# Sharing one run of 64x64 matmuls between two batches in linear attention followed by a two-layer MLP

## The chip, the cores and the metric

The kernel runs on one core of one Trainium2 chip. The metric is device time in microseconds (us), of one launch from start to end. A core has five engines that run side by side and wait for one another through semaphores: TensorE (PE in the profile; its weight loads are PEld), VectorE (DVE), ScalarE (ACT), GpSimd (POOL) and SyncE (SP). Here SP issues most of the DMAs, in program order. Matmul results go to PSUM, which the kernel uses as eight banks of 128 partitions by 512 fp32 values. The operands lie in SBUF.

## The reference: what is computed

There are 8 batches and 8 heads, 576 positions, and a head size of 64. First comes linear attention, then a two-layer MLP with a leaky ReLU:

```python
q_s = softmax(q, over d)          # over the 64 values of a position
k_s = softmax(k, over s)          # over the 576 positions of a head
kv  = einsum('bhsd,bhse->bhde', k_s, v)
x   = einsum('bhsd,bhde->bhse', q_s, kv)     # then 4608 tokens x 512
h   = x @ w_in                               # 512 -> 2048
out = maximum(0.01 * h, h) @ w_out           # 2048 -> 512
```

q, k, v, both weights and the result are float32. The kernel multiplies in bf16.

## The kernel before

**MLP.** The 4608 tokens are cut into nine tiles of 512 (t = 0 to 8). In tiles 1 to 8 the first layer has 16 steps j. Each has four matmuls of 512 columns (448 in tile 1) into one bank `ph` (`layer1`, L462), and ACT's Prelu (`leaky`, L471) makes the bf16 tile `gj` of it. The second layer has four sub-tiles of 128 tokens, each of 16 matmuls (`layer2`, L483) into one bank `pout`. DVE copies it to `out_sb` (L477; ACT does so for two sub-tiles of tile 1), and SP stores it with two DMAs (L480). `pout` has two banks (`psO`) and `out_sb` four buffers. All other PSUM tiles, `ph`, `pkv` and `po`, take turns in six banks (`psB`).

**Attention of one batch.** These are the steps:

- `load_all` (L505) issues three DMAs of 1152 KB on SP, for k, q and v. They go to `raw` buffers, of which there are six, enough for two batches. A load has to wait until its buffer was read for the last time.
- `k_tree` (L152) and `k_allmax` (L157 to L177), both on DVE, find the maxima of k over the positions. `k_sub` (L185, POOL) subtracts them and `k_exp` (L193, ACT) writes `ke`.
- `q_max` (L217, DVE), `q_sub` (L248, POOL), `q_exp` (L256, ACT), `q_sum` (L265 and L267, DVE) and `q_norm` (L272, DVE) make the softmax of q. `q_turn` (L430) transposes it by a DMA that SP issues, into `qX`.
- `v_cast` (L205, POOL, twice) writes v as bf16 into `vb`, beside a column of ones that gives the sum for k's softmax.
- `kv` (L286): 72 matmuls in 64x64 pieces of the array, with 65 columns each, into the two banks `pkv`. Row half hh writes bank hh.
- `kd_make` (L304 and L305): DVE takes a reciprocal and multiplies, twice, and leaves `kd` in SBUF.
- `attend_x` (L435): 16 matmuls in 64x64 pieces (`quads`, L411). Part 0 has five of the nine position groups, 320 columns in four banks, and part 1 the other four, 2 x 256 columns in two banks. ACT then casts the six banks into `xT` (`move`, L402), part 0 first. `xT` is the input of the first layer.

**Order of the work.** The order is written out by hand. `at(t, u, ...)` (L494) hangs steps on unit u of tile t, and `run(t, u)` (L499) issues them there. Units 0 to 15 are the steps of the first layer, and units 16 to 31 are groups of four matmuls of the second. A unit of 32 or more goes on into the next tile. So a unit stands for four matmuls of 512 columns. Each engine works through its own list in this order and waits only for its data and buffers. The store of a sub-tile is issued just ahead of the steps on its last unit, 19, 23, 27 or 31.

Batches 0 and 1 have an order of their own, and `plan2` that of batch 2. `plan(b, o)` (L604) serves batches 3 to 7: it starts in tile b - 2 at unit o, which is 27 for batch 3, 22 for batch 4 and 17 for the others. Counted in tiles, `kv(3)` stands at unit 20 of tile 2 and `attend_x(3)` at unit 29 there. For batch 4 these are units 15 and 25 of tile 3, and for batches 5 to 7 units 10 and 20 of tile b - 1. Tile b is the first to read the tokens of batch b, for b from 3 to 7. The loads of batch b stand at unit 2 of tile b - 2.

Of the kernel before, what the change touches and what calls it, by code (L numbers as in the profile page):

```python
# [8 lines left out]
FP32 = mybir.dt.float32  # L9
# [16 lines left out]
def kernel(  # L26
# [9 lines left out]
    nc = tc.nc  # L36
# [3 lines left out]
    B, H, S, D = q.shape  # L40
# [6 lines left out]
    P = 128  # L47
# [19 lines left out]
    psB_pool = ctx.enter_context(tc.tile_pool(name="psB", bufs=6, space=bass.MemoryType.PSUM))  # L67
    psO_pool = ctx.enter_context(tc.tile_pool(name="psO", bufs=2, space=bass.MemoryType.PSUM))
    BANK_TAG = "bank2k"


    def load(src, b, name, cuts):

        t = raw_pool.tile([P, HL, R, D], FP32, name=name, tag="raw")
        flat = src[b].rearrange("h s d -> (h s d)").rearrange(
            "(hl p r d) -> p hl r d", hl=HL, p=P, r=R
        )
        for hs, rs in cuts:
            nc.sync.dma_start(
                out=t[:, hs, rs].rearrange("p h r d -> p h (r d)"),  # L80
                in_=flat[:, hs, rs].rearrange("p h r d -> p h (r d)"),
            )
        return t

    ALLH, ALLR = slice(0, HL), slice(0, R)
# [47 lines left out]
    def k_begin(b):  # L133
        st[b]["ke"] = ke_pool.tile([P, R, HL, D], BF16, name="ke")
        st[b]["kmax"] = mx_pool.tile([P, HL, D], FP32, name="kmax")
        st[b]["kmaxT"] = mx_pool.tile([P, HL * D], FP32, name="kmaxT")
        st[b]["kall"] = mx_pool.tile([P, HL, D], FP32, name="kall")
# [16 lines left out]
    def k_allmax(b):  # L154


        nc.vector.transpose(  # L157
            out=st[b]["kmaxT"], in_=st[b]["kmax"].rearrange("p h d -> p (h d)")
        )
        m2 = small_pool.tile([P, CB, 2], FP32, name="m2")  # L160
        nc.vector.tensor_reduce(
            out=m2[:, :, 0],
            in_=st[b]["kmaxT"].rearrange("p (c j) -> p c j", j=32),
            axis=AX.X,
            op=ALU.max,
        )
        for a in range(4):
            o = a ^ 1
            nc.vector.tensor_reduce(
                out=m2[32 * o : 32 * o + 32, :, 1],  # L170
                in_=m2[32 * a : 32 * a + 32, :, 0:1],
                axis=AX.X,
                op=ALU.max,
            )
        m = small_pool.tile([P, CB], FP32, name="m")
        nc.vector.tensor_reduce(out=m, in_=m2, axis=AX.X, op=ALU.max)
        nc.vector.transpose(  # L177
            out=st[b]["kall"].rearrange("p h d -> p (h d)"),
            in_=m.unsqueeze(2).to_broadcast([P, CB, 32]),
        )  # L180

    def k_sub(eng, b, hs):
        ks = st[b]["k"][:, hs]
        n = hs.stop - hs.start
        eng.tensor_tensor(  # L185
            out=ks,
            in0=ks,
            in1=st[b]["kall"][:, hs].unsqueeze(2).to_broadcast([P, n, R, D]),
            op=ALU.subtract,
        )  # L190
# [17 lines left out]
    def q_begin(b):  # L208
        st[b]["qe"] = qe_pool.tile([P, R, HL, D], BF16, name="qe")
        if b == 0:  # L210
            for gg in range(2):
                st[b]["qT", gg] = qT_pool.tile([P, 2, R, L], BF16, name=f"qT{gg}", tag="qT")

    def q_max(b, rs):
        n = rs.stop - rs.start
        st[b]["qmax", rs.start] = m = small_pool.tile([P, HL, n], FP32, name="qmax")
        nc.vector.tensor_reduce(out=m, in_=st[b]["q"][:, :, rs], axis=AX.X, op=ALU.max)  # L217
# [62 lines left out]
    def kv_half(b, gg, outs):  # L280

        for r in range(R):
            for hh in range(2):
                rows = slice(hh * L, (hh + 1) * L)
                for hp in range(2):
                    nc.tensor.matmul(  # L286
                        outs[hh][hp * D : (hp + 1) * D],
                        lhsT=st[b]["ke"][rows, r, 2 * gg + hp],
                        rhs=vb2[b % 2][rows, r, 2 * gg + hp, 0 : D + 1],
                        start=(r == 0),  # L290
                        stop=(r == R - 1),
                    )

    def kv(b):
        pkv = [psB_pool.tile([P, 2, 66], FP32, name="pkv", tag=BANK_TAG) for _ in range(2)]
        for gg in range(2):
            kv_half(b, gg, [p[:, gg, 0 : D + 1] for p in pkv])
        st[b]["pkv"] = pkv

    def kd_make(b):  # L300
        for hh in range(2):
            pkv = st[b]["pkv"][hh]
            krec = small_pool.tile([P, 2, 1], FP32, name="krec")
            nc.vector.reciprocal(out=krec, in_=pkv[:, :, D : D + 1])  # L304
            nc.vector.tensor_tensor(  # L305
                out=kd2[b % 2][:, 2 * hh : 2 * hh + 2],
                in0=pkv[:, :, 0:D],
                in1=krec.to_broadcast([P, 2, D]),
                op=ALU.mult,
            )  # L310
# [89 lines left out]
    def move(eng, o, i):  # L400
        if eng is nc.scalar:
            eng.copy(out=o, in_=i)  # L402
        else:
            eng.tensor_copy(out=o, in_=i)

    def quads(b, gg, ps, src, shape=None):

        for hp in range(2):
            for hh in range(2):
                o = ps[hp][hh * D : (hh + 1) * D]  # L410
                nc.tensor.matmul(  # L411
                    o if shape is None else shape(o),
                    lhsT=kd2[b % 2][hp * D : (hp + 1) * D, 2 * hh + gg],
                    rhs=src(hh)[hp * D : (hp + 1) * D],
                    start=True,
                    stop=True,
                )
# [14 lines left out]
            in_=st[b]["qe"][:, rs].rearrange("p r h d -> p (r h d)"),  # L432
        )

    def attend_x(b, parts, engs):  # L435

        qX = st[b]["qX"].rearrange("c (r g) (h l) -> c g h r l", g=2, h=2)
        made = []
        for i in parts:
            rs = XR[i]  # L440
            n = (rs.stop - rs.start) * L
            cols = slice(b * S + rs.start * L, b * S + rs.stop * L)
            per = 512 // n
            for g0 in range(0, 2, per):
                ps = [psB_pool.tile([P, per, n], FP32, name="po", tag=BANK_TAG) for _ in range(2)]
                for gg in range(g0, g0 + per):
                    quads(
                        b,
                        gg,
                        [p[:, gg - g0] for p in ps],  # L450
                        lambda hh: qX[:, gg, hh, rs],
                        lambda o: o.rearrange("p (r l) -> p r l", l=L),
                    )
                for hp in range(2):
                    c = 2 * g0 + hp
                    made.append((xT[:, c : c + 2 * per - 1 : 2, cols], ps[hp]))
        for i, (o, p) in enumerate(made):
            move(engs[i % len(engs)], o, p)
# [35 lines left out]
    def at(t, u, *fns):  # L494
        while t > 0 and u >= 32:
            t, u = t + 1, u - 32
        hooks.setdefault((t, u), []).extend(fns)
# [7 lines left out]
    def load_all(b):  # L505
        whole = [(ALLH, ALLR)]
        st[b]["k"] = load(k, b, "k_raw", whole)
        st[b]["q"] = load(q, b, "q_raw", whole)
        st[b]["v"] = load(v, b, "v_raw", whole)
# [87 lines left out]
    for i in range(2):  # L597
        at(0, (45, 46)[i], lambda i=i: attend_x(1, (i,), (nc.scalar, nc.vector)))


    for b in range(3, B):
        at(b - 2, 2, lambda b=b: load_all(b))

    def plan(b, o):  # L604
        t = b - 2
        at(t, o, lambda: k_begin(b), lambda: q_begin(b), lambda: k_tree(b, ALLH))
        at(t, o + 3, lambda: k_allmax(b), lambda: k_sub(nc.gpsimd, b, ALLH))
        at(t, o + 7, lambda: q_max(b, ALLR), lambda: q_sub(nc.gpsimd, b, ALLR))
        at(t, o + 11, lambda: k_exp(b, ALLH))
        at(t, o + 12, lambda: v_cast(nc.gpsimd, b, 0), lambda: v_cast(nc.gpsimd, b, 1))  # L610
        at(t, o + 16, lambda: q_exp(b, ALLR))
        at(t, o + 18, lambda: q_sum(b, ALLR))
        at(t, o + 21, lambda: q_norm(b, ALLR))
        kvu, pu = o + 25, o + (33 if b == 3 else 34)
        at(t, kvu, lambda: kv(b))
        at(t, kvu + 1, lambda: kd_make(b))
        at(t, o + 22, lambda: q_turn(b))
        at(t, pu + 1, lambda: attend_x(b, (0, 1), (nc.scalar,)))


    def plan2():
# [15 lines left out]

    plan2()
    for b in range(3, B):
        plan(b, {3: 27, 4: 22}.get(b, 17))  # L640


    def g_tile():
# [57 lines left out]
    for t in range(1, NT):  # L701
# [9 lines left out]
        for tsub in range(NTS):  # L711
            row0 = t * TT + tsub * P
            if row0 == T - P:
                for os, copy in ((slice(0, 384), nc.scalar.copy), (slice(384, O), nc.vector.tensor_copy)):
                    po = psB_pool.tile([P, os.stop - os.start], FP32, name="pout2", tag=BANK_TAG)
# [4 lines left out]
            po = psO_pool.tile([P, O], FP32, name="pout")  # L720
# [37 lines left out]
```

## Time and profile before

| what | value |
|---|---|
| time, median of 3 runs | 285.16 us (284.78 to 285.27) |
| the profiled execution's own time | 284.93 us |
| its span, first to last instruction | 283.1 us |
| TensorE clock granted | 1.00 over the span |
| DMA | 46.38 MB, 164 GB/s on average |
| matmuls of layer 1 (L462) | 628 in the trace, 126.8 us busy |
| matmuls of layer 2 (L483) | 579 in the trace, 126.0 us busy |
| kv (L286) | 576 matmuls, 6.5 us busy |
| attend by qX (L411) | 112 matmuls, 269 to 320 ns each by the model |

The span is what the instructions take; the rest of the profiled execution's time lies around it. In the first tile of the profile TensorE also computes matmuls on zeros (L316), 26 of them. The layers have 640 and 592 weight loads (PEld) in the trace, so a few matmul records are missing there; a hole of about 0.216 us between two matmuls with no releaser is such a record. Where a view lists a group, the columns are busy time, the mean of one in ns, and the idle time of the engine just before, with what ended it. In a timeline the first column is the start within the span, and the second the length of a merged group.

The tiles begin, by the first L462 of each, at 50.49 (tile 1), 78.21, 107.53, 136.72, 165.90, 195.06, 224.23 and 251.85 us (tile 8).

### The profile page before, as it was taken

To read this page: it belongs to the slowest core of one execution; us is meant where nothing else is said; L and a number is where in the kernel's file an instruction comes from. 1 tells how busy PE (TensorE), PEld (TensorE's weight loads), DVE (VectorE), ACT (ScalarE), POOL (GpSimd) and SP (SyncE) were. 2 spreads that over 40 slices of the span, in tenths; PEclk is the share of its full clock that TensorE was granted. 3 is DMA by queue.
4 is the path that set the end of the run, shared out by engine and by line. 5 is a ranking of instruction groups with operands and counts; after the bars stand their busy time and mean duration, and the time that the engine had idled before them with its cause. 6 is when DMAs were issued, how large, how long until landed. Compare 5 with 4: busy or idle time off the path is not lost.

```text
span 283.1 us, 4910 instructions
## 1 busy us (share of the span) xinstructions
PE 272.0 (96%) x1967; PEld 131.4 (46%) x1994; DVE 143.6 (51%) x232; ACT 146.0 (52%) x262; POOL 82.7 (29%) x61
## 2 busy tenths in 40 slices
PE   7699899999999999999999999999999999999995
PEld 2277644554444444444444444444444444444443
DVE  3996794987860992597193718472711100110011
ACT  4977881685269208914773367435843165016400
POOL 2523651026078029307800690059000000000000
PEclk9999999999999999999999999999999999999999
DMA  7998999999959166953597349923061310230033
GB/s 251 331 211 313 296 194 165 400 311 355 175 130 411 45 147 157 407 93 74 116 397 150 74 81 380 200 65 80 5 86 39 80 32 0 59 80 13 0 74 74
DMA packets 38870, 46.38 MB, mean 164 GB/s; under 512 B 18240, under 2 KB 21568, under 8 KB 38848
## 3 DMA queue, kind: packets, MB, share of 16 engines
q1 hardware_dynamic: 35456, 41.75, 52.1%
q0 software_dynamic: 3232, 4.19, 8.4%
q8 instruction: 15, 0.25, 0.4%
q10 hardware_dynamic: 160, 0.13, 0.1%
q14 instruction: 7, 0.06, 0.1%
HBM read 36.70 MB, written 9.44 MB: 163 GB/s over the span
## 4 chain that ended last, share of the span: by engine, by line
PE 86%; DMA 7%; issue 1%; DVE 1%; POOL 0%; SPq 0%; POOLq 0%
PE pout L483 44%; PE ph L462 38%; DMA w_out_sb<-in_moe_w_out_dram 3%; DMA w_in_sb<-in_moe_w_in_dram 2%; PE pkv L286 2%; DMA k_raw<-in_k_dram 2%; PE po L411 2%; DVE k_raw L353 1%; SPq L515 0%; POOL gate L580 0%; DVE out_sb L477 0%; POOL gate L547 0%; POOLq L580 0%; POOLq L547 0%
## 5 line engine op out<-in xcount | busy, mean ns | idle before, releaser
L483 PE MATMUL pout<-w_out_sb,gj 128*128 128x512 bf16 (+2 forms) x579 | 126.0, 373 | 2.0 <-issue 1.0
L462 PE MATMUL ph<-xT,w_in_sb 128*128 128x512 bf16 (+3 forms) x628 | 126.8, 357 | 0.9 <-DMA w_in_sb<-in_moe_w_in_dram 0.2
L471 ACT ACTIVATE gj<-ph 128x512 bf16<-128x512 f32 (+2 forms) x152 | 83.5, 581 | 55.5 <-PE ph L462 52.6
L462 PEld LDWEIGHTS <-w_in_sb 128*128 128x128 bf16 x640 | 62.1, 98 | 62.5 <-issue 0.9
L483 PEld LDWEIGHTS <-gj 128*128 128x128 bf16 x592 | 56.2, 98 | 67.0 <-issue 2.8
L477 DVE COPY out_sb<-pout 128x512 f32<-128x512 f32 (+1 forms) x34 | 22.7, 676 | 88.1 <-PE pout L483 66.0
L185 POOL TENSOR_TENSOR k_raw<-k_raw,kall 128x2304 f32<-128x2304 f32 x5 | 25.4, 5070 | 73.8 <-DVE kall L177 44.4
L402 ACT CAST xT<-po 128x320 bf16<-128x320 f32 (+2 forms) x45 | 17.8, 487 | 47.1 <-PE po L411 47.1
L248 POOL TENSOR_TENSOR q_raw<-q_raw,qmax 128x2304 f32<-128x2304 f32 (+3 forms) x10 | 29.7, 2978 | 21.5 <-DMA out_dram<-out_sb 15.4
L265 DVE TENSOR_REDUCE qsum<-qe 128x36 f32<-128x2304 bf16 (+4 forms) x11 | 19.8, 1797 | 30.7 <-ACT qe L256 30.7
L193 ACT ACTIVATE ke<-k_raw 128x2304 bf16<-128x2304 f32 (+2 forms) x11 | 17.5, 1595 | 9.6 <-POOL k_raw L185 9.6
L272 DVE TENSOR_TENSOR qe<-qe,qrec 128x2304 bf16<-128x2304 bf16 (+4 forms) x12 | 21.9, 1826 | 0.4
L217 DVE TENSOR_REDUCE qmax<-q_raw 128x36 f32<-128x2304 f32 (+4 forms) x11 | 19.6, 1791 | 1.4 <-DMA q_raw<-in_q_dram 1.4
L256 ACT ACTIVATE qe<-q_raw 128x2304 bf16<-128x2304 f32 (+4 forms) x11 | 16.8, 1527 | 0.9 <-POOL q_raw L248 0.8
L205 POOL CAST vb<-v_raw 128x1152 bf16<-128x1152 f32 x13 | 14.6, 1153 | 0.0
L152 DVE TENSOR_TENSOR t<-k_raw 128x1024 f32<-128x1024 f32 (+1 forms) x10 | 10.1, 1006 | 0.9 <-DMA k_raw<-in_k_dram 0.7
L152 DVE TENSOR_TENSOR t<-t 128x256 f32<-128x256 f32 (+2 forms) x20 | 9.6, 478 | 0.6
L316 PE MATMUL pout<-zero 128*128 128x512 bf16 x26 | 8.4, 453 | 1.3 <-POOL zero L101 1.3
L477 ACT COPY out_sb<-pout 128x512 f32<-128x512 f32 (+1 forms) x3 | 1.6, 543 | 14.2 <-PE pout L483 14.2
L286 PEld LDWEIGHTS <-ke 64*64 64x64 bf16 x576 | 5.5, 106 | 4.4 <-ACT gj L471 1.7
L286 PE MATMUL pkv<-vb,ke 64*64 64x65 bf16 x576 | 6.5, 194 | 0.8 <-ACT vb L203 0.8
L230 ACT ACTIVATE qe<-q_raw,nmax 128x64 bf16<-128x64 f32 x16 | 5.3, 333 | 3.3 <-DVE nmax L225 3.3
(53 smaller groups left out, 85.8 us busy)
## 6 DMA issues: line engine op xcount, KB each, us to landing
out_dram<-out_sb SPq DMA_DIRECT2D x70, 128.0 KB, 2.4
q_raw<-in_q_dram SPq DMA_DIRECT2D x7, 1152.0 KB, 8.6
v_raw<-in_v_dram SPq DMA_DIRECT2D x7, 1152.0 KB, 11.5
k_raw<-in_k_dram SPq DMA_DIRECT2D x6, 1152.0 KB, 6.1
k_raw<-in_k_dram SPq DMA_DIRECT2D x4, 576.0 KB, 5.2
w_in_sb<-in_moe_w_in_dram POOLq DMA_DIRECT2D x4, 512.0 KB, 7.7
v_raw<-in_v_dram SPq DMA_DIRECT2D x2, 576.0 KB, 7.2
w_out_sb<-in_moe_w_out_dram POOLq DMA_DIRECT2D x4, 256.0 KB, 9.4
```

What stands on the lines that cost most here:

```text
L152: nc.vector.tensor_tensor(out=o, in0=i0, in1=i1, op=ALU.max)
L185: eng.tensor_tensor(out=ks, in0=ks, in1=st[b]["kall"][:, hs].unsqueeze(2).to_broadcast([P, n, R, D]), op=ALU.subtract,)
L217: nc.vector.tensor_reduce(out=m, in_=st[b]["q"][:, :, rs], axis=AX.X, op=ALU.max)
L248: eng.tensor_tensor(out=qs, in0=qs, in1=st[b]["qmax", rs.start].unsqueeze(3).to_broadcast([P, HL, n, D]), op=ALU.subtract,)
L265: nc.vector.reduce_sum(out=qsum, in_=st[b]["qe"][:, rs], axis=AX.X)
L272: nc.vector.tensor_tensor(out=qes, in0=qes, in1=st[b]["qrec", rs.start].unsqueeze(3).to_broadcast([P, n, HL, D]), op=ALU.mult,)
L286: nc.tensor.matmul(outs[hh][hp * D : (hp + 1) * D], lhsT=st[b]["ke"][rows, r, 2 * gg + hp], rhs=vb2[b % 2][rows, r, 2 * gg + hp, 0 : D + 1 ...
L402: eng.copy(out=o, in_=i)
L462: nc.tensor.matmul(ph, lhsT=w_in_sb[:, i, j * P : (j + 1) * P], rhs=xT[:, i, c0 : c0 + n], start=(i == 0 and first), stop=(i == NB - 1 and ...
L471: nc.scalar.activation(out=o, in_=ph, func=AF.Prelu, alpha=LEAKY_SLOPE)
L477: copy(out=out_sb, in_=pout)
L483: nc.tensor.matmul(pout, lhsT=g_sb[j // 2][:, j % 2, tsub * P : (tsub + 1) * P], rhs=w_out_sb[:, j, os], start=(j == 0), stop=(j == NF - 1),)
```

## The change

The products of keys and values of batch b + 1 are issued within `attend_x` of batch b, ahead of its quads, for b = 3 to 6. They lie in the same two banks as the first pair of `po`: columns 0 to 319 hold the query products and columns 320 to 451 hold `pkv`. `attend_x` of batches 3 to 7 stands at unit 29 of tile b - 1, and `kd_make` of the next batch one unit later. `kv(3)` keeps its own place. The preparation of batches 4 to 7 begins at unit 4 of tile b - 2; batch 3 keeps unit 27 of tile 1. The k_sub of batch 4 is on DVE, all four heads in one instruction, and no longer on POOL. The loads of batches 4 to 7 stand at unit 18 of tile 1, unit 12 of tile 2, unit 24 of tile 3 and unit 24 of tile 4.

```diff
-    def kv(b):
-        pkv = [psB_pool.tile([P, 2, 66], FP32, name="pkv", tag=BANK_TAG) for _ in range(2)]
+    def kv(b, pkv=None):
+        if pkv is None:
+            pkv = [psB_pool.tile([P, 2, 66], FP32, name="pkv", tag=BANK_TAG) for _ in range(2)]
...
-    def attend_x(b, parts, engs):
+    def attend_x(b, parts, engs, kv_next=None):
...
-                ps = [psB_pool.tile([P, per, n], FP32, name="po", tag=BANK_TAG) for _ in range(2)]
+                banks = [psB_pool.tile([P, 512], FP32, name="po", tag=BANK_TAG) for _ in range(2)]
+                ps = [p[:, 0 : per * n].rearrange("p (g n) -> p g n", g=per) for p in banks]
+                if kv_next is not None and not pkv:
+                    pkv = [p[:, n : n + 132].rearrange("p (g e) -> p g e", g=2) for p in banks]
+                    kv(kv_next, pkv)
...
     for b in range(3, B):
-        at(b - 2, 2, lambda b=b: load_all(b))
+        at(*{3: (1, 2), 4: (1, 18), 5: (2, 12)}.get(b, (b - 3, 24)), lambda b=b: load_all(b))
...
-        at(t, o + 3, lambda: k_allmax(b), lambda: k_sub(nc.gpsimd, b, ALLH))
+        at(t, o + 3, lambda: k_allmax(b), lambda: k_sub(nc.vector if b == 4 else nc.gpsimd, b, ALLH))
...
-        kvu, pu = o + 25, o + (33 if b == 3 else 34)
-        at(t, kvu, lambda: kv(b))
-        at(t, kvu + 1, lambda: kd_make(b))
+        if b == 3:
+            at(t, o + 25, lambda: kv(b))
+            at(t, o + 26, lambda: kd_make(b))
         at(t, o + 22, lambda: q_turn(b))
-        at(t, pu + 1, lambda: attend_x(b, (0, 1), (nc.scalar,)))
+        after = None if b == B - 1 else b + 1
+        at(b - 1, 29, lambda: attend_x(b, (0, 1), (nc.scalar,), after))
+        if after:
+            at(b - 1, 30, lambda: kd_make(after))
...
-        plan(b, {3: 27, 4: 22}.get(b, 17))
+        plan(b, 27 if b == 3 else 4)
```

More of the change, by code (lines that the diff above doesn't have):

```diff
@@ L433, in q_turn @@
         )
-    def attend_x(b, parts, engs):
+    def attend_x(b, parts, engs, kv_next=None):
         qX = st[b]["qX"].rearrange("c (r g) (h l) -> c g h r l", g=2, h=2)
-        made = []
+        made, pkv = [], []
         for i in parts:
```

## The prediction

> **What bounds the kernel now.** First the page's busy row, then the table of TensorE's waits (total us, times, longest):
>
> ```profile
> PE 272.0 (96%) x1967; PEld 131.4 (46%) x1994; DVE 143.6 (51%) x232; ACT 146.0 (52%) x262; POOL 82.7 (29%) x61
> ```
>
> ```profile
> PE pout L483 <- issue: 1.0, 6, 0.2
> PE kT L327 <- DVE kmax L152: 0.8, 1, 0.8
> PE pkv L286 <- ACT vb L203: 0.8, 1, 0.8
> ```
>
> TensorE is busy 96% of the span. Its waits are short: "issue" is no wait for another engine, and the others, on lines of batch 0's own attention, belong to the start-up. So after the first tile only TensorE's own stream can be shortened. Next the windows, one per token tile (tiles 2 to 5, and tile 7, which carries no attention):
>
> ```profile
> 78.20:107.50 29.30, 28.88 (x213) 13.43 (x216) 19.59 (x32) 14.86 (x25) 14.30 (x5) 1.00 0.61 182
> 107.50:136.70 29.20, 28.94 (x214) 13.43 (x216) 16.13 (x24) 17.43 (x26) 16.00 (x6) 1.00 0.63 179
> ...
> 224.20:251.90 27.70, 27.54 (x127) 12.55 (x129) 2.77 (x4) 9.55 (x16) 0.00 (x0) 1.00 0.17 38
> ```
>
> The first number behind the stretch is its length, then busy time of PE, PEld, DVE, ACT, POOL, and the clock, 1.00 everywhere. A tile with one kv and one attend takes 1.5 us longer (29.2 against 27.7), and that is all that attention costs after the start. The timeline splits it:
>
> ```profile
> 95.61 1.03 PE L483 MATMUL pout<-w_out_sb,gj 128*128 128x512 bf16 x4
> ...
> 96.56 0.69 PEld L286 LDWEIGHTS <-ke 64*64 64x64 bf16 x72 [0.42 <-issue]
> 96.56 0.81 PE L286 MATMUL pkv<-vb,ke 64*64 64x65 bf16 x72
> ...
> 97.30 0.76 PEld L483 LDWEIGHTS <-gj 128*128 128x128 bf16 x5
> ```
>
> ```profile
> 105.17 0.68 PE L411 MATMUL po<-qX,kd 64*64 64x320 bf16 x16
> 105.54 2.39 ACT L402 CAST xT<-po 128x320 bf16<-128x320 f32 x6 [11.89 <-PE po L411]
> ...
> 107.53 1.24 PE L462 MATMUL ph<-xT,w_in_sb 128*128 128x512 bf16 x5
> ```
>
> Matmul starts are measured and ends modelled, so I work with starts. The four L483 ahead of kv(3) start 0.216 us apart, the last at 96.26; the first kv matmul follows it by 0.309. **Entering** a run of 64x64 matmuls thus costs 0.309 - 0.216 = 0.093 us; the other kv and attend runs of tiles 1 to 6 give 0.093 or 0.094. The last kv matmul starts at 97.16 and the next 128x128 weight load at 97.30, 0.14 us later; in the runs of batches 5 to 7 the next matmul comes 0.126 to 0.144 after the last one. Less 0.027 for its own 65 columns (0.216 x 65/512), **leaving** costs 0.10 to 0.12. Leaving an attend costs 0.09 (0.20 us from the last 256-column matmul of batch 2, less 0.108). No engine appears as a releaser in these places: what is lost is the change of shape itself.
>
> **Part 1: kv of the next batch within attend_x.** The counts of matmuls, weight loads, casts and DVE steps stay: 72 matmuls for each kv (0.81 us), 16 for each attend (0.68 us). For batches 4 to 7 kv has no run of its own now: it stands ahead of attend of batches 3 to 6. Removed are four exits from kv (0.10 to 0.12) and four entries to attend (0.093), some 0.2 us each: 4 x 0.20 = **0.8 us less on TensorE**. The seam inside the run, kv's last matmul to attend's first, has no row of before that is free of another wait (batch 0 goes from L286 to L411, but there TensorE waited for ACT). From below it is one more step of kv's own rhythm, 0.034 us for four matmuls (72 of them start within 0.593 us), which costs nothing extra; from above a full exit and entry, 0.2 us, which would eat the gain. I take the lower end, since both sides are 64x64 matmuls and the two attend groups within a run also change tile and bank without any such gap (starts 0.135 us apart for 320 columns, which is their streaming time). Both ends stay in the range.
>
> The Trainium skill has a rule that could speak against sharing the banks: "TensorEngine Tiling (Array Packing)", Gotcha 1, says that different row tiles can't write one PSUM bank at the same time. In kv row half hh writes bank hh and in quads row half hp writes bank hp, the same pairing, so by that rule too the seam needs no pause; were they crossed, the sum would be 0 in place of -0.8 us. No run here shows the crossed case.
>
> **Part 2: what the shared banks wait for.** The first two banks are now free only when kd_make has read them as well. One row tells how two readers of one bank are ordered:
>
> ```profile
> L398 DVE COPY qT<-psum_qt 128x384 bf16<-128x384 bf16 x1 | 0.4, 357 | 1.0 <-ACT qT L396 1.0
> ```
>
> DVE waited for ACT's copy out of the same bank, though their halves differ. So kd_make, issued behind the moves, should wait for ACT's first cast (in before 105.54 to 105.96, so 0.80 us after attend's first matmul at 105.17), and then takes 0.16 + 0.03 + 0.29 us for the first bank: done at +1.3. The next tile's first layer-1 matmul starts at +2.36 (107.53 less 105.17): cover 1.0 us, cost nothing. The second bank is needed one 0.86 us step later. Queued behind kd_make on DVE is only the last out_sb copy, due about when layer 1 starts. The Trainium skill's "PSUM — Partial Sum Buffer", section on bank collisions, asks for that guard by bank and not by address; the row agrees, and its 1.0 us is a wait for one whole copy.
>
> **Part 3: attend at unit 29.** For batches 4 to 7 it moves from units 20 to 25 to eight matmuls before the next layer 1. Batch 3 stands there already: its first four casts (part 0, all that the next tile reads) end at 106.95, before layer 1 at 107.53, and no wait appears. Cost nothing, cover 0.6 us. Where kv sat within layer 1 (batches 5 to 7) it took two of six banks; no wait showed there, so none goes.
>
> **Part 4: loads and preparation sooner.** In tiles 3 to 5 DVE has 16 us of work in 29, and 10 us or more lie between the last of k_exp and v_cast and the kv that needs them. Loads of batches 4 and 5 go out 9 us or more ahead of their first use. Batch 6's, at unit 24 of tile 3 and behind a store on SP, go out near 131.5, and its k_tree is due near 138: whole k loads landed 5.8 to 7.6 us after issue, so it is just in time, and its k_sub on POOL would end 3 us before ACT comes to k_exp; batch 7 likewise. On SP these loads precede stores and q_turn: transposes took 3.9 to 6.9 us to land, some behind a load, and from batch 4 on the consumer is a tile later; delayed stores hold four out_sb buffers that are next asked for some 15 us later. All hidden; without that cover a late load costs what it exceeds 3 us by.
>
> Tile 2 is different: batches 3 and 4 are both prepared in it, by DVE:
>
> ```profile
> 80.27 2.53 DVE L217 TENSOR_REDUCE qmax<-q_raw 128x36 f32<-128x2304 f32 x1
> 91.73 2.55 DVE L265 TENSOR_REDUCE qsum<-qe 128x36 f32<-128x2304 bf16 x1 [8.93 <-ACT qe L256]
> ```
>
> Those 8.93 us of idle time take in batch 4's k_tree (2.9 from start to last step), k_allmax (2.3), k_sub (2.55, an estimate: q_max's 2.53 for the same 2304 elements) and q_max (2.45): from 82.72 to 92.84. q_sum of batch 3 starts 1.1 us later than before, its q_norm ends at 98.4, the first out copy at 99.0, kd_make(3) at 99.8. Then q_sum(4), 2.95 with its reciprocal, and only then the second out copy, ending near **103.3**. TensorE needs that copy's pout bank for its fourth sub-tile: tile 2's first L483 at 92.16, plus 48 x 0.2158, plus kv(3)'s 0.83, is **103.34**. It is on the edge: I put 0.05 us there. q_norm(4), the third copy and kd_make(4) then end near 107.3, before layer 1 at some 108.3. q_turn(3) goes out at 98.6 behind batch 5's loads; even with the longest landing (6.9) it is there at 105.5, before attend(3) at 106.0. ACT and POOL keep pace: q_sub(4) ends near 97.2, k_exp(4) near 94.7, v_cast(4) near 99.4, and kv(4) comes at 105.4.
>
> **Sum.** -0.8 + 0.05 = -0.75 us. The profiled execution of 284.93 (span 283.1, 1.8 around it) becomes 284.2; it lay 0.23 below the median of 285.16, so I forecast the median as **284.4**. A measurement of this kernel tells about 0.2% (0.57 us) from no change, so even the full gain is just over that bound.
>
> **Rivals.**
> - DVE late in tile 2 (slower). Each us that the second copy ends past 103.34 stops TensorE for a us; from 1.3 us of slip (0.75 and 0.57) the kernel is slower. For it: 22 us of DVE work without a gap. Against: DVE's durations are the same with POOL busy (k_sub 1351 to 1359 ns) and k(4), landing near 80.7, is 2 us early. At 2 us of slip, 286.4; at 0.8, no change. Chance 0.20.
> - kd_make late in four tiles (slower). If it waits for all six casts, it begins at +2.76, ends its first half at +3.3, and layer 1 starts 0.95 late: 4 x 0.95 - 0.8 = +3.0, 288.2. The row above has a wait for the same bank alone, which speaks against it. Chance 0.08.
> - The change doesn't do what it says: the seam costs an exit and an entry. No gain: 285.1. Chance 0.17.
> - Forecast, 0.55, its own range 284.1 to 284.7.
>
> Faster by over 0.2%: 0.45 of the forecast's 0.55. Within: 0.09 of it, 0.16 of the seam, 0.05 of late DVE, 0.30. Slower: late DVE 0.15, kd_make 0.08 and 0.02 of the rest, 0.25. The range reaches to a DVE slip of 1.6 us (286.0), and down to 283.9 for a larger exit.
>
> **What will show it.** TensorE's timeline: four runs with L286 x72 and L411 x16 together and no L483 or L462 between; one 0.309 entry each. Tiles 3 to 5 shorter by 0.2 us, to 29.0. A wait of L483 for DVE out_sb near 103 to 104 us shows the first rival, a wait of L462 for DVE kd at a tile's start the second. Wrong would be any new releaser of TensorE in tiles 1 to 6.

## The result

The changed kernel takes **293.89 us** (median of 5 runs, 293.26 to 294.82) against 285.16: the ratio is 1.032, with a 95% interval of 1.030 to 1.034. Forecast were 284.4, and 283.9 to 286.0 as the range. The profiled execution took 293.26 us, with a span of 291.5.

First TensorE's waits in the changed kernel (total us, times, longest). `layer2` is L488 in its numbering, `layer1` L467 and `quads` L412; L286 and the lines ahead of it are unchanged.

```profile
PE pout L488 <- DVE out_sb L482: 7.7, 1, 7.7
```

There is one new wait: a matmul of the second layer waited 7.7 us, once, for DVE's copy out of a `pout` bank. That is the place of the first rival, tile 2, though at its first copy and not at the second. The windows by tile, 2, 3 and 6, show that the whole loss lies there:

```profile
78.00:117.30 39.30, 31.60 (x289) 14.47 (x288) 36.88 (x40) 19.20 (x27) 21.46 (x7) 0.91 0.70 221
117.30:146.40 29.10, 29.10 (x218) 13.59 (x217) 15.95 (x24) 16.04 (x25) 11.26 (x4) 1.00 0.39 100
...
204.30:232.60 28.30, 28.30 (x145) 12.80 (x144) 2.77 (x4) 11.88 (x23) 0.00 (x0) 1.00 0.23 52
```

Tile 2 grew from 29.3 to 39.3 us, tiles 3 to 5 fell from 29.2 us to between 28.9 and 29.1, and tile 6, which lost a kv to tile 5, is 28.3. DVE is busy for 36.88 us of tile 2, and 8.5 us of that is new: no instruction came on top of the list that was forecast, but k_tree got 7.4 us longer and q_norm 1.1. The timeline of DVE in tile 2:

```profile
80.07 2.53 DVE L217 TENSOR_REDUCE qmax<-q_raw 128x36 f32<-128x2304 f32 x1
82.53 3.33 DVE L152 TENSOR_TENSOR t<-k_raw 128x1024 f32<-128x1024 f32 x1
85.89 5.71 DVE L152 TENSOR_TENSOR t<-t 128x512 f32<-128x512 f32 x2
91.63 1.25 DVE L152 TENSOR_TENSOR kmax<-t,k_raw 128x256 f32<-128x256 f32 x1
...
103.22 3.69 DVE L272 TENSOR_TENSOR qe<-qe,qrec 128x2304 bf16<-128x2304 bf16 x1
106.83 0.68 DVE L482 COPY out_sb<-pout 128x512 f32<-128x512 f32 x1
```

and of POOL in the same stretch:

```profile
79.71 5.07 POOL L185 TENSOR_TENSOR k_raw<-k_raw,kall 128x2304 f32<-128x2304 f32 x1 [11.21 <-issue]
84.74 5.03 POOL L248 TENSOR_TENSOR q_raw<-q_raw,qmax 128x2304 f32<-128x2304 f32 x1
89.71 2.90 POOL L205 CAST vb<-v_raw 128x1152 bf16<-128x1152 f32 x2
100.45 4.05 POOL L248 TENSOR_TENSOR q_raw<-q_raw,qmax 128x2304 f32<-128x2304 f32 x1 [7.84 <-issue]
```

In the kernel before, the same four maxima stood here, and POOL was idle for 13.29 us ahead of the last line:

```profile
98.61 1.22 DVE L152 TENSOR_TENSOR t<-k_raw 128x1024 f32<-128x1024 f32 x1
99.86 1.15 DVE L152 TENSOR_TENSOR t<-t 128x512 f32<-128x512 f32 x2
101.04 0.43 DVE L152 TENSOR_TENSOR kmax<-t,k_raw 128x256 f32<-128x256 f32 x1
...
104.45 5.07 POOL L185 TENSOR_TENSOR k_raw<-k_raw,kall 128x2304 f32<-128x2304 f32 x1 [13.29 <-DVE kall L177]
```

The four maxima of k_tree (L152) took 10.3 us from first start to last end, where before they took 2.9. The reduction beside the same POOL work kept its 2.53. Read the ends in the changed kernel: k_sub on POOL ends at 84.78, and the first maximum at 85.86, which is 1.08 us later and nearly its own length. POOL's q_sub was issued at 84.74, runs 0.97 us longer than the 4.06 of before, and ends at 89.77. The next maximum, 0.69 us alone, ends at 90.31, just behind it. The two engines take turns, and each waits for the whole of the other's instruction. The profile counts that wait as busy time, with no idle time and no releaser.

The wait also cost TensorE its clock for a while:

```profile
107.56 4.69 PE L488 MATMUL pout<-w_out_sb,gj 128*128 128x512 bf16 x14 [7.70 <-DVE out_sb L482]
```

Fourteen matmuls behind the wait span 4.69 us. Start to start, six of them take 0.427 us in place of 0.216 and two are in between. That is 1.5 us more, and the clock of the tile is 0.91. So tile 2 loses 7.9 us to the wait (8.08 from start to start, less 0.22) and 1.5 to the clock. From the start of tile 2 to that of tile 7 the kernel went from 146.02 to 154.61 us, 8.6 us more, which leaves 0.8 us gained elsewhere.

### The profile page after: what moved, and what is told of

It is laid out like the page before. It is cut to its first block, busy times and chain, and to the rows that moved or that the text cites. A ratio compares the mean times of both kernels' runs of the same rounds, so it can differ in the third digit from the quotient of the medians.

```text
span 291.5 us, 4935 instructions
## 1 busy us (share of the span) xinstructions
PE 275.6 (95%) x1994; PEld 132.1 (45%) x1994; DVE 154.0 (53%) x233; ACT 148.9 (51%) x262; POOL 81.7 (28%) x60
## 4 chain that ended last, share of the span: by engine, by line
PE 75%; DVE 11%; DMA 7%; issue 2%; POOL 1%; SPq 0%; DVEq 0%; POOLq 0%
PE pout L488 39%; PE ph L467 33%; DVE t L152 4%; DMA w_out_sb<-in_moe_w_out_dram 3%; DMA w_in_sb<-in_moe_w_in_dram 2%; DVE qmax L217 2%; DMA k_raw<-in_k_dram 1%; PE po L412 1%; PE po L286 1%; DVE k_raw L185 1%; DVE qsum L265 1%; DVE out_sb L482 1%; DVE k_raw L354 1%; DVE kmax L152 1%; PE pkv L286 0%
## 5 line engine op out<-in xcount | busy, mean ns | idle before, releaser
L488 PE MATMUL pout<-w_out_sb,gj 128*128 128x512 bf16 (+2 forms) x592 | 129.7, 377 | 8.0 <-DVE out_sb L482 7.7
L467 PE MATMUL ph<-xT,w_in_sb 128*128 128x512 bf16 (+3 forms) x640 | 126.9, 358 | 0.1
L476 ACT ACTIVATE gj<-ph 128x512 bf16<-128x512 f32 (+2 forms) x152 | 85.6, 575 | 49.5 <-PE ph L467 47.9
L488 PEld LDWEIGHTS <-gj 128*128 128x128 bf16 x592 | 56.8, 99 | 75.7 <-issue 12.4
L467 PEld LDWEIGHTS <-w_in_sb 128*128 128x128 bf16 x640 | 62.3, 98 | 63.0 <-issue 0.9
L248 POOL TENSOR_TENSOR q_raw<-q_raw,qmax 128x2304 f32<-128x2304 f32 (+3 forms) x10 | 30.7, 3076 | 30.3 <-DVE qmax L217 22.4
L185 POOL TENSOR_TENSOR k_raw<-k_raw,kall 128x2304 f32<-128x2304 f32 x4 | 20.3, 5068 | 61.1 <-DVE kall L177 35.4
L272 DVE TENSOR_TENSOR qe<-qe,qrec 128x2304 bf16<-128x2304 bf16 (+4 forms) x12 | 23.0, 1916 | 0.3
L205 POOL CAST vb<-v_raw 128x1152 bf16<-128x1152 f32 x13 | 17.6, 1384 | 0.0
L152 DVE TENSOR_TENSOR t<-t 128x256 f32<-128x256 f32 (+2 forms) x20 | 14.1, 706 | 0.6
L152 DVE TENSOR_TENSOR t<-k_raw 128x1024 f32<-128x1024 f32 (+1 forms) x10 | 12.2, 1218 | 0.4 <-DMA k_raw<-in_k_dram 0.2
L317 PE MATMUL pout<-zero 128*128 128x512 bf16 x28 | 9.1, 454 | 1.3 <-POOL zero L101 1.3
L185 DVE TENSOR_TENSOR k_raw<-k_raw,kall 128x1152 f32<-128x1152 f32 (+1 forms) x5 | 7.8, 1595 | 0.2
L286 PEld LDWEIGHTS <-ke 64*64 64x64 bf16 x576 | 5.6, 106 | 4.4 <-issue 2.5
## 6 DMA issues: line engine op xcount, KB each, us to landing
v_raw<-in_v_dram SPq DMA_DIRECT2D x7, 1152.0 KB, 11.4
```

Of the source, the lines that this page charges most:

```text
L152: nc.vector.tensor_tensor(out=o, in0=i0, in1=i1, op=ALU.max)
L185: eng.tensor_tensor(out=ks, in0=ks, in1=st[b]["kall"][:, hs].unsqueeze(2).to_broadcast([P, n, R, D]), op=ALU.subtract,)
L248: eng.tensor_tensor(out=qs, in0=qs, in1=st[b]["qmax", rs.start].unsqueeze(3).to_broadcast([P, HL, n, D]), op=ALU.subtract,)
L272: nc.vector.tensor_tensor(out=qes, in0=qes, in1=st[b]["qrec", rs.start].unsqueeze(3).to_broadcast([P, n, HL, D]), op=ALU.mult,)
L467: nc.tensor.matmul(ph, lhsT=w_in_sb[:, i, j * P : (j + 1) * P], rhs=xT[:, i, c0 : c0 + n], start=(i == 0 and first), stop=(i == NB - 1 and ...
L476: nc.scalar.activation(out=o, in_=ph, func=AF.Prelu, alpha=LEAKY_SLOPE)
```

## Experiments

The theory: a DVE instruction that reads two SBUF tiles, and a POOL instruction that reads SBUF, wait for each other for whole instructions, so k_tree of batch 4 stands behind POOL's work on batch 3, and behind it the copy that TensorE needs. The rivals: DVE's list in tile 2 was simply mis-added; the loads slow DVE; the order of the copies alone is wrong; or the shared runs gain nothing. In the diffs `-` is the kernel named, `+` the experiment.

**1. A first probe, on the kernel before.**

```diff
+    def dve_list():
...
+        nc.vector.tensor_tensor(out=t4, in0=ks[:, :, 0:4], in1=ks[:, :, 4:8], op=ALU.max)
+        q_max(7, ALLR)
+        nc.vector.tensor_copy(out=t4, in_=ks[:, :, 0:4])
+        nc.vector.tensor_tensor(out=t4, in0=ks[:, :, 0:4], in1=ks[:, :, 4:8], op=ALU.max)
```

> The kernel before with added instructions in tiles 7 and 8, where no attention is left; they only touch buffers that nobody reads any more. DVE runs one list three times: a maximum of two SBUF tiles (128x1024 fp32, two inputs), a reduction over one tile (128x2304), a copy of one tile (128x1024), and the two-input maximum again. In tile 7 POOL runs four subtractions of 128x2304 (q_sub) beside it, in tile 8 first nothing and then four fills of 128x2304. Theory (a DVE step with two SBUF inputs stands still for the whole of a POOL instruction that reads SBUF): beside q_sub each two-input maximum takes what is left of a running subtraction more, so 2 to 5.2 us in place of 1.22; the reduction keeps 2.53; beside the fills the maximum keeps 1.22. Rival (DVE was slowed by the DMA traffic or by its own list): the maxima stay at 1.22 beside POOL too. The Trainium skill, SBUF — State Buffer, section Who interferes with whom, states the rule of the theory, and that a copy in a two-port mode contends as well; by that the copy would be stretched beside q_sub.

Inconclusive, by a fault in the list: q_max reads what q_sub writes, so DVE waited for POOL by its data (16.32 us idle, released by q_sub) and ran nearly all the rest alone. (The added work makes it 298.39 us, in one run.) One thing stood: the first maximum began 0.23 us ahead of the first q_sub, and that q_sub took 4.89 us, where the next three took 4.05. POOL waits for DVE as well.

**2. The changed kernel without the subtractions of batch 3.** No other experiment leaves out a part of the computation.

```diff
-        at(t, o + 3, lambda: k_allmax(b), lambda: k_sub(nc.vector if b == 4 else nc.gpsimd, b, ALLH))
-        at(t, o + 7, lambda: q_max(b, ALLR), lambda: q_sub(nc.gpsimd, b, ALLR))
+        at(t, o + 3, lambda: k_allmax(b), *([] if b == 3 else [lambda: k_sub(nc.vector if b == 4 else nc.gpsimd, b, ALLH)]))
+        at(t, o + 7, lambda: q_max(b, ALLR), *([] if b == 3 else [lambda: q_sub(nc.gpsimd, b, ALLR)]))
```

> The changed kernel without the two subtractions of batch 3 on POOL: its softmaxes are computed without taking the maxima off first. DVE's list in tile 2 is the same, instruction for instruction. Theory (DVE's two-input steps of batch 4 stood behind POOL's k_sub and q_sub of batch 3, and the out_sb copy behind them): k_tree of batch 4 takes 2.9 us from first start to last end, or up to some 4 where a v_cast is met, in place of 10.3; the wait of L488 for DVE out_sb falls from 7.7 us to under 1; the time is 284.4 to 285.6. Rival (the list of DVE in tile 2 is simply too long, and was mis-added): the wait stays at 4 us or more, and the time at 289 or more. Rival (loads of batch 4 slow DVE): k_tree stays at 8 us or more, since the loads are the same.

285.06 us, a ratio of 1.0006 (0.9993 to 1.0019). DVE's list is unchanged, and its timeline begins as the forecast had it:

```profile
82.72 1.21 DVE L152 TENSOR_TENSOR t<-k_raw 128x1024 f32<-128x1024 f32 x1
83.96 1.15 DVE L152 TENSOR_TENSOR t<-t 128x512 f32<-128x512 f32 x2
85.15 0.42 DVE L152 TENSOR_TENSOR kmax<-t,k_raw 128x256 f32<-128x256 f32 x1
...
95.85 3.69 DVE L272 TENSOR_TENSOR qe<-qe,qrec 128x2304 bf16<-128x2304 bf16 x1
```

k_tree takes 2.9 us again, and the wait for out_sb is 0.6 us. So the list was not too long by itself, and batch 4's loads, which are the same, don't slow DVE: both rivals fall. q_norm still met a q_sub on POOL (issued at 93.07, 4.05 long), is 1.1 us longer than alone, and ended the second out copy at 104.4, not at 103.3. That wait, 0.8 us from start to start, just ate the gain.

**3. k_tree of batch 4 as one reduction, with POOL's list untouched.**

```diff
+        if b == 4:
+            nc.vector.tensor_reduce(
+                out=st[b]["kmax"][:, hs],
+                in_=st[b]["k"][:, hs].rearrange("p h r d -> p h d r"),
+                axis=AX.X,
+                op=ALU.max,
+            )
+            return
```

> The changed kernel with k_tree of batch 4 as one DVE reduction over positions, an instruction with one SBUF input, in place of four maxima of two inputs. POOL's list is the same. Theory (two-input steps behind POOL): the reduction takes 2.5 us although POOL runs all the while; k_sub and q_norm still have two inputs and lose 1 to 2 us each; L488 waits 1 to 3 us in all for out_sb, no half-speed matmuls follow, and the time is 286 to 288. Rival (any DVE instruction is slowed beside POOL or the loads): the reduction is stretched to 5 us or more and the time stays above 290.

287.08 us, a ratio of 1.0068 (1.0051 to 1.0085). TensorE waited 2.5 us in two waits for out_sb, and no half-speed matmuls followed. The reduction took 4.20 us, not 2.5; the second probe tells why. k_sub and q_norm lost 0.6 and 1.1 us, where 1 to 2 each were expected. Only k_tree of batch 4 was changed, from four instructions with two SBUF inputs to one with one, and 6.8 us came back.

**4. The first two out copies of tile 2 on ACT.**

```diff
-                    store(row0, po, nc.scalar.copy if t == 1 and tsub < 2 else nc.vector.tensor_copy)
+                    store(row0, po, nc.scalar.copy if t in (1, 2) and tsub < 2 else nc.vector.tensor_copy)
```

> The changed kernel with the first two out_sb copies of tile 2 on ACT in place of DVE. It takes away what L488 waited for and nothing else. Theory (DVE's whole chain of tile 2 is late, and the copy was only the first to tell): DVE stays as late, k_exp and q_exp of batch 4 are in ACT's list ahead of the copies, so L488 still waits some 1 us and some 3 us for ACT, then kv for v_cast near 109 and attend(3) for q_turn(3) near 111; the time is 289.5 to 292. Rival (the order of the copies on DVE is all that is wrong): the time falls to 284.4 to 286.

290.35 us in one run. The waits moved on:

```profile
PE pout L488 <- ACT out_sb L482: 3.7, 2, 3.0
...
PE po L412 <- DMA qX<-qe: 1.2, 1, 1.2
```

The out copy was only the first to tell. Behind it the whole chain of batches 3 and 4 is late: q_turn(3), and kd_make(4), for which the next layer 1 waits 0.7 us. The wait for v_cast that was expected didn't come.

**5. A second probe, without that fault.** The list no longer reads what POOL writes; there are reductions (`one()`) between the other steps, a product of two bf16 inputs, and a reduction whose elements lie 64 apart.

```diff
+        one()
+        nc.vector.tensor_tensor(out=t4, in0=ks[:, :, 0:4], in1=ks[:, :, 4:8], op=ALU.max)
+        one()
+        nc.vector.tensor_copy(out=t4, in_=ks[:, :, 0:4])
+        one()
+        nc.vector.tensor_tensor(out=qe, in0=qe, in1=qe, op=ALU.mult)
+        one()
+        nc.vector.tensor_reduce(
+            out=st[7]["kmax"], in_=ks.rearrange("p h r d -> p h d r"), axis=AX.X, op=ALU.max
+        )
```

> The kernel before with a list of DVE instructions added three times in its last tiles, on buffers that nobody reads any more: reductions of 128x2304 with one SBUF input, and between them a maximum of two SBUF tiles (1024 elements), a copy of one (1024), a product of two bf16 inputs (2304), and at the end a reduction whose innermost step is 64 elements apart (2304). Beside it POOL does nothing, then eight subtractions of 128x2304 (q_sub), then eight fills of the same size. In the first probe the list waited for POOL by its data; here it doesn't. Theory (a DVE step with two SBUF inputs, and a POOL instruction that reads SBUF, wait for each other for whole instructions): alone the steps take 2.53, 1.22, 0.68, 2.55 and, for the last, 2.5 or, if the spacing costs, 4.2 us. Beside q_sub the maximum and the product take their own time and what is left of a subtraction, 1.2 to 5.3 and 2.6 to 6.6 us, and the subtraction that is in POOL's list behind them is longer than 4.05 by their own time or less; the reductions stay as alone. Beside fills all stay as alone, but perhaps the copy. Rival (DVE is slowed evenly beside POOL): all steps are longer by one factor.

The run took 316.16 us with the added work. In order of time: alone (L664 at 229.72), beside q_sub (at 249.05), and beside fills (at 286.89). Columns are start and length.

```profile
229.72 1.22 DVE L664 TENSOR_TENSOR t<-k_raw 128x1024 f32<-128x1024 f32 x1
...
249.05 2.90 DVE L664 TENSOR_TENSOR t<-k_raw 128x1024 f32<-128x1024 f32 x1
251.87 2.54 DVE L661 TENSOR_REDUCE one<-k_raw 128x36 f32<-128x2304 f32 x1
254.33 2.07 DVE L666 COPY t<-k_raw 128x1024 f32<-128x1024 f32 x1
...
258.78 2.73 DVE L668 TENSOR_TENSOR qe<-qe 128x2304 bf16<-128x2304 bf16 x1
...
286.89 1.22 DVE L664 TENSOR_TENSOR t<-k_raw 128x1024 f32<-128x1024 f32 x1
```

The maximum takes 1.22 us alone, 2.90 beside a POOL instruction that reads SBUF, and 1.22 beside one that only writes. The product goes from 1.35 (2.55 had been expected) to 2.73, and the copy, which has one input, from 0.68 to 2.07. All twelve reductions lie between 2.535 and 2.548 us. The spaced one, which makes 256 results of nine values each where the others make 36 of 64, takes 4.06 to 4.10 in all three places, so in experiment 3 its form cost the time and not POOL. The subtractions behind a stretched step took 4.4 to 5.0 us, the others 4.05. An even slowing would have met the reductions too: that rival falls.

The Trainium skill says just this: "SBUF — State Buffer", section "Who interferes with whom", has a DVE instruction with two SBUF inputs and a GpSimd instruction that reads SBUF block each other for a whole instruction, and reductions never. Runs 2, 3 and 5 agree with it, with the numbers above. It was the rule to weigh in the prediction.

**6 and 7. A version that takes the pile-up out of tile 2, and its control.** The new version, on the changed kernel, keeps the shared runs. k_tree(4) is as in experiment 3 and the out copies are as in experiment 4. The rest, for batches 4 to 7 with t = b - 2:

```diff
-        at(*{3: (1, 2), 4: (1, 18), 5: (2, 12)}.get(b, (b - 3, 24)), lambda b=b: load_all(b))
+        at(*{3: (1, 2), 4: (1, 18), 5: (2, 12)}.get(b, (b - 3, 4)), lambda b=b: load_all(b))
...
+            if b > 4:
+                at(t, 3, lambda: v_cast(nc.gpsimd, b, 0), lambda: v_cast(nc.gpsimd, b, 1))
...
+            if b == 4:
+                at(t, 16, lambda: v_cast(nc.scalar, b, 0), lambda: v_cast(nc.scalar, b, 1))
+            at(t, 22, lambda: q_max(b, ALLR), lambda: q_sub(nc.gpsimd, b, ALLR))
+            at(t, 31, lambda: q_exp(b, ALLR))
+            at(t + 1, 1, lambda: q_sum(b, ALLR))
+            at(t + 1, 2, lambda: q_norm(b, ALLR))
+            at(t + 1, 3, lambda: q_turn(b))
```

> A version of the changed kernel that keeps the shared runs and takes the pile-up out of tile 2: k_tree of batch 4 is one reduction; v_cast of batch 4 and the first two out_sb copies of tile 2 are on ACT; for batches 4 to 7 q_max comes at unit 22, q_exp after the casts of attend, and q_sum, q_norm and q_turn go out in the next tile; v_cast comes early on POOL and the loads of batches 6 and 7 at unit 4. Theory (the shared runs gain 0.8 us, and all else was the pile-up): no wait of L488 for out_sb in tile 2 over 0.2 us, four shared runs, and the time is 0.6 to 0.9 us below that of before, 284.2 to 284.5. Rival (the shared runs gain nothing that lasts): within 0.2 us of before.

The control takes the sharing out again, and kv and kd_make go four units ahead of attend for it:

```diff
-        at(b - 1, 29, lambda: attend_x(b, (0, 1), (nc.scalar,), after))
+        at(b - 1, 29, lambda: attend_x(b, (0, 1), (nc.scalar,)))
...
-            at(b - 1, 30, lambda: kd_make(after))
+            at(b - 1, 25, lambda: kv(after))
+            at(b - 1, 26, lambda: kd_make(after))
```

> The version of e6_best with kv of batches 4 to 7 in a run of its own and in banks of its own again, four units ahead of attend, and kd_make behind it. All else is as in e6_best. Theory: four more entries and exits of 64x64 runs, each pair some 0.2 us: 0.8 us slower than e6_best, within 0.2 us of before. Rival (sharing the run is worth nothing): the same time as e6_best.

291.84 and 292.22 us: both expectations missed. No wait for out_sb was left, but another came in its place. TensorE's longest wait in experiment 6, and SP's timeline:

```profile
PE po L420 <- DMA qX<-qe: 4.9, 1, 4.9
```

```profile
93.33 0.39 SPq L79 DMA_DIRECT2D k_raw<-in_k_dram  x1
...
94.37 0.45 SPq L79 DMA_DIRECT2D v_raw<-in_v_dram  x1
97.82 9.12 SPq L439 DMA_TRANSPOSE qX<-qe  x1
```

The loads of batch 5 stand ahead of q_turn(3) on SP. They went out only when v_cast(3) had ended on POOL at 93.30, the v load landed at 107.0, and q_turn(3), issued at 97.82, landed at 110.6, 12.8 us later. In the changed kernel this could not show: q_norm was late, so q_turn(3) was issued only at 106.97, when these loads had landed (the last at 104.96), and took 4.0 us.

**8 and 9. The same two, with batch 5's loads behind q_turn(3).**

```diff
-        at(*{3: (1, 2), 4: (1, 18), 5: (2, 12)}.get(b, (b - 3, 4)), lambda b=b: load_all(b))
+        at(*{3: (1, 2), 4: (1, 18), 5: (2, 18)}.get(b, (b - 3, 4)), lambda b=b: load_all(b))
```

> The version of e6_best with one thing moved: the loads of batch 5 stand at unit 18 of tile 2, behind q_turn(3) in SP's list, and no longer at unit 12 ahead of it. In e6_best no out_sb wait was left, but attend(3) waited 4.9 us for q_turn(3), which went out at 97.8 while batch 5's loads filled the DMA queue (v landed at 107.0) and landed at 110.6. Theory: q_turn(3) lands near 102 again, no wait of 0.2 us or more is left in tiles 2 to 6, and the time is 0.6 to 0.9 us below that of before. Rival (the DMAs are late for another reason, or the shared runs gain nothing): a wait for a DMA or within 0.2 us of before.

> The version of e8_best with kv of batches 4 to 7 in a run and banks of its own, four units ahead of attend, and kd_make behind it. Theory: four more exits and entries of 64x64 runs, 0.8 us slower than e8_best and within 0.2 us of before. Rival (sharing a run is worth nothing): the same time as e8_best.

Shared: 284.56 us, a ratio of 0.9971 to before (0.9960 to 0.9983). Apart: 285.51 us, 1.0008 (0.9996 to 1.0020). The windows of tiles 2 to 6, shared and then apart, end in these sums:

```profile
sum 145.30, PE 143.94 PEld 67.38 DVE 81.85 ACT 80.49 POOL 53.88; mean PE 28.79 PEld 13.48 DVE 16.37 ACT 16.10 POOL 10.78
```

```profile
sum 146.30, PE 144.93 PEld 67.32 DVE 81.93 ACT 80.49 POOL 51.55; mean PE 28.99 PEld 13.46 DVE 16.39 ACT 16.10 POOL 10.31
```

The first number is the length: 1.0 us between them, for four exits and entries. Some 0.1 us of it is that one more kv run is spread in experiment 9 (see the end of the next section). Neither has a wait of TensorE from tile 2 on that is as long as 0.2 us. So the shared runs do gain, and the version of experiment 8 is faster than both kernels, by 0.3% in the case of the kernel before.

## Why the prediction was wrong, point by point

- **Part 1, the shared runs: right.** The seam costs nothing. In the changed kernel the first quad starts 0.009 to 0.025 us after the last kv matmul, and the two are one run with one entry of 0.309:

```profile
172.39 0.78 PE L286 MATMUL po<-vb,ke 64*64 64x65 bf16 x72
172.98 0.68 PE L412 MATMUL po<-qX,kd 64*64 64x320 bf16 x16
```

  The size was about 0.22 us for a pair and not 0.20. In the changed kernel, from the start of the last 128x128 matmul ahead to that of the first behind, kv(3) alone takes 1.045 us, attend(7) alone 0.926, and the shared run of tile 2 takes 1.538: 1.045 + 0.926 - 1.538, less the usual step of 0.216, is 0.22. Four of them are 0.9 us, and the spread kv run makes it the 1.0 between experiments 8 and 9.
- **Part 2, kd_make behind ACT's cast: right.** The wait is there, and it has cover: kd_make ended at 116.7, and the next layer 1 began at 117.31 with no wait. That rival can be struck; in experiment 4 layer 1 did wait 0.7 us for kd, but there DVE's own list was late.

```profile
115.81 0.17 DVE L305 RECIPROCAL krec<-po 128x2 f32<-128x2 f32 x1 [1.02 <-ACT xT L403]
```

- **Part 3, attend at unit 29: right.** The tiles' first L467 follow without a wait.
- **Part 4, the step that failed: "Tile 2 is different", with k_tree at 2.9 us, and the argument under the first rival, "DVE's durations are the same with POOL busy (k_sub 1351 to 1359 ns)".** The rival was named, with its place, the bank and the price of 1 us for 1 us, but it was given 0.20 on that argument, and the argument was false. Two of these k_sub ran from 34.48 to 37.1, and POOL was idle from 34.61 to 38.33; the other two ran from 57.97 to 60.59, and POOL was idle until 62.07. The durations agreed because POOL was not busy. Where DVE and POOL did meet in the trace of before, the rows said the opposite. First DVE, then POOL, around 68 us:

```profile
67.57 2.21 DVE L272 TENSOR_TENSOR qe<-qe,qrec 128x1280 bf16<-128x1280 bf16 x1
```

```profile
66.21 2.23 POOL L205 CAST vb<-v_raw 128x1152 bf16<-128x1152 f32 x2
```

  The same product took 1.59 us at 39.98. And at 40.17 a POOL copy of 128x128, 0.29 us elsewhere, took 1.55 beside that one. Before, this cost little: k_tree(4) came at 98.6, when POOL had nothing. The change put it under 11.4 us of POOL's work (5.07, 4.06 and 2.24). Measured: k_tree 10.3 us in place of 2.9, and q_norm of batch 3 3.69 in place of 2.56. With 7.4 + 1.1 us of delay, the first out copy, due at 99.0 by the forecast and needed by TensorE at 99.7, ended at 107.5.
- **A term that was missing: the clock.** Each us of slip was priced at one us. A wait of 7.9 us cost 9.4.
- **Part 4, "even with the longest landing (6.9)": wrong, but not what decided.** A transpose that was next behind three loads in SP's list took 12.8 us to land in experiment 6, and 13.4 and 12.8 in tiles 3 and 4 of the changed kernel, where it had the time.
- **Part 4, "It is on the edge":** right. In experiment 2 the 1.1 us that q_norm lost were enough to make 0.8 us of wait at that second copy, and the time is that of before.

What stays open: kv runs that are spread over 0.67 to 0.72 us where 0.58 to 0.59 is usual, in one tile of the changed kernel, two of experiment 8 and three of experiment 9. The extra time is one or two gaps behind the 60th of the 72 matmuls; what they meet was not found. It is worth some 0.1 us each.

## What to carry to other kernels

Before work is moved under another engine, look for the rows in which the two already meet, by start and end, and not by their mean durations: such a wait stands in the busy time, and only a longer instruction shows it. Count the instructions with two SBUF inputs on DVE, and its copies, against what POOL reads at that time; where they must meet, a reduction gets by (2.54 us in all places), or ACT (k_exp took 2.12 us beside POOL's q_sub at 85 us, as elsewhere). And when one long wait is removed, expect the next one: here a late transpose came where the late copy had been.

## What the runs showed of the hardware beyond that

- A copy from SBUF to SBUF on DVE has one input and still waited for POOL's subtraction (0.68 to 2.07 us). Beside a fill it took 0.81, and a fill 2.44 in place of 2.02. The Trainium skill, "SBUF — State Buffer", section "Who interferes with whom", has a copy in a two-port mode contend with GpSimd. The rows agree, though none names the mode.
- Waits of 3.1 us and less (experiments 3 and 4) left TensorE's matmuls at 0.216 us. After 3.9, 4.9 and 7.9 us (experiments 7 and 6, the changed kernel) 8 to 11 of them took up to 0.427, and 1.5 to 2.4 us were lost on top (the granted clock was 0.50 from 110 to 115 us of experiment 6): without a late transpose and that loss, 291.84 became 284.56. "TensorE: Matmul & The Clock Gate" of the Trainium skill, Part 1, puts the idle window behind which the clock is halved at about 3.4 us. The runs lie on both sides of it and agree.
- A reduction to 256 results of nine values that lie 64 apart takes 1.6 times as long as one to 36 results of 64 neighbours (4.1 and 2.54 us for the same 2304 elements). Whether the spacing or the short rows cost it, no run shows.
